# First product of the second feed-forward part by Strassen's scheme over two of its three input blocks

## The chip, the cores and the metric

The kernel runs on one core of a Trainium2 chip (trn2). The metric is the time of one execution on the device in microseconds; the time of a kernel is the median of its runs. Engines have the profile's short names: PE is the matrix engine TensorE, PEld its weight loads, DVE is VectorE, ACT is ScalarE, POOL is GpSimd, SP is SyncE, which issues the DMA transfers here.

## What is computed

A recurrent attention (4 sequences, 8 heads, 768 steps, 48 channels a head) gives 3072 tokens of 384 channels. A gated feed-forward part and a second one with Mish follow:

```python
def _moe_ref(x, w_gate, w_val, w_out) -> np.ndarray:
    gate = 1.0 / (1.0 + np.exp(-(x @ w_gate)))
    val = x @ w_val
    return (gate * val @ w_out).astype(np.float32)
...
def _moe2_ref(x, w_in, w_out) -> np.ndarray:
    h = x @ w_in
    sp = np.where(h > 20.0, h, np.log1p(np.exp(np.minimum(h, 20.0))))
    g = h * np.tanh(sp)
    return (g @ w_out).astype(np.float32)
```

The first part's weights are 384x1536 (twice) and 1536x384, the second's are 384x2048 (`w_in`) and 2048x384 (`w_out`).

## The kernel before

Every fp32 product is made of three fp16 ones: each factor is split into a high half and a rest, and high x high, high x rest and rest x high are summed in PSUM. The weights lie in DRAM as 64-bit words and are decoded on the chip into the two halves; the decoding of a chunk (`load_raw`, `decode`, L329) is a transfer, a few integer steps on ACT and DVE (L306, L350), a cast for the high half (L361) and a subtraction for the rest (L364). For `w_out` of the second part, `combine` (L378) also makes sums and differences of its blocks (L389), because that product already follows Strassen's scheme.

**First part.** It runs over 12 pairs (NP) of 256 tokens (NT). While attention for a later pair is computed on all engines, `gate` (L1116) makes the gate and value products of a pair (L1133), the sigmoid (L1144), their product (L1149) and its split (L1161, L1164), and `out1` (L1190) the next product (L1201). Its results go to DRAM as `x2d`, split in two halves.

**Second part.** It runs over 6 blocks (RB) of 512 tokens, two pairs each. `load_x2` fetches a block. `h_unit` (L1298) makes one column of 128 of the first product with 9 matmuls of 128x512 (3 input blocks x 3 terms, L1311) from weights that stay in SBUF, and ACT applies Mish to it in one step (L1322). There are 16 such units per block. `operands` (L1328) takes two of them and makes what the second product needs: four sums on POOL (L1345), and seven operands that `split2` splits into a high half on ACT (L1359) and a rest on DVE (L1364). `out2` (L1401) is the second product by Strassen's scheme, 14 units of 24 matmuls of 128x192 per block (L1426), each with an evacuation on ACT or DVE (L1439, L1441). In block 0 the units of the first product alternate with the last pair's `out1` units; later with the `out2` units of the block before.

**What sets the order.** All work is registered as tasks with engines, costs in microseconds, and keys that they read and write. The class `Plan` gives each a due time, worked out backwards from the end, and a simulated clock then hands each engine the ready task that is due first (`run`, L115; `schedule`, L140). The result is a fixed order per engine; at run time each engine, SP's DMA queue among them, goes through its own list and waits on semaphores. `tail_end` (L1568) registers the decoding of the second part's weights; before, the chunks of `w_in` are decoded near the end of the first part, those of `w_out` across the border between the parts. The main loop is at L1599 to L1648.

## Time and profile before

| | before |
|---|---|
| median of 3 runs | 918.23 us (917.8 to 918.44) |
| profiled execution | 919.56 us |
| its span in the profile | 917.8 us |
| PE busy | 866.2 us, 94% |
| DVE busy | 633.6 us, 69% |
| POOL busy | 506.4 us, 55% |
| ACT busy | 490.7 us, 53% |

The span is what the profile covers; 1.76 us of the profiled execution lie around it, and this execution is 1.33 us above the median. Matrix products overlap their own filling and draining, so the duration shown for one matmul is longer than its distance to the next; prices are read from pieces of a chain instead.

### The profile page before, as it was taken

Reading aid. Unit: us, or ns where it says so; the run is one execution under the profiler, and the core shown is the slowest. Engines: PE = TensorE matmul, PEld = TensorE weight load, DVE = VectorE, ACT = ScalarE, POOL = GpSimd, SP = SyncE. Lnnn points to the kernel's source line nnn. Section 1 sums busy time; section 2 is a strip of 40 time slices with the busy share of each in tenths; the row PEclk is TensorE's granted clock in tenths of the full one; section 3 lists DMA queues with packets and bytes.
Section 4 is the critical chain, followed back from the end, with each engine's and each line's share of the span. In section 5 each row is a group of like instructions: output and inputs, shape, how many; then the busy total and the mean of one; then the engine's idle time right before and its main releaser. Section 6 shows DMA issues by size and latency. Waiting matters only on the chain.

```text
span 917.8 us, 29861 instructions
## 1 busy us (share of the span) xinstructions
PE 866.2 (94%) x13064; PEld 701.3 (76%) x13064; DVE 633.6 (69%) x1098; ACT 490.7 (53%) x1125; POOL 506.4 (55%) x562
## 2 busy tenths in 40 slices
PE   0578899999999999999999999999999999999998
PEld 0456788888888888888888885577677676776788
DVE  7897898877585777767688768765655655556541
ACT  2687854363543525262548777764655655556540
POOL 7996976646557474847553476543533434335320
PEclk9998999999999999999999999999999999999999
DMA  9277633222322232332306910100101002000001
GB/s 333 88 240 250 226 102 101 69 71 71 99 84 60 80 87 75 69 91 54 79 23 189 260 47 13 43 5 10 61 1 46 25 1 70 1 27 10 2 35 36
DMA packets 55315, 74.29 MB, mean 81 GB/s; under 512 B 19600, under 2 KB 36496, under 8 KB 55056
## 3 DMA queue, kind: packets, MB, share of 16 engines
q1 hardware_dynamic: 55184, 72.38, 26.3%
q8 instruction: 102, 1.67, 0.8%
q14 instruction: 29, 0.24, 0.1%
HBM read 58.99 MB, written 9.44 MB: 75 GB/s over the span
## 4 chain that ended last, share of the span: by engine, by line
PE 85%; POOL 4%; DVE 4%; ACT 3%; DMA 2%; issue 1%; SPq 0%; DVEq 0%; ACTq 0%; POOLq 0%
PE gv L1133 27%; PE h L1311 20%; PE o L1426 18%; PE o L1201 14%; PE yp L1013 3%; POOL pt L546 2%; PE kp L910 2%; POOL blk L546 1%; ACT KK L851 1%; ACT X L716 1%; PE lp L695 1%; POOL wos L364 1%; DMA raw_wv<-wv 1%; DVE A L566 1%; PE kt L806 0%
## 5 line engine op out<-in xcount | busy, mean ns | idle before, releaser
L1311 PE MATMUL h<-x,wis 128*128 128x512 f16 x864 | 199.9, 379 | 0.0
L1345 POOL TENSOR_TENSOR sum<-e 128x256 f32<-128x256 f32 x96 | 71.9, 748 | 179.9 <-ACT e L1322 179.9
L1133 PE MATMUL gv<-xt,wgs 128*128 128x256 f16 x1296 | 166.5, 274 | 4.8 <-DVE gt L1164 3.1
L1133 PE MATMUL gv<-xt,wvs 128*128 128x256 f16 x1296 | 165.6, 275 | 2.1 <-ACT sig L1144 1.8
L1201 PE MATMUL o<-gt,wos 128*128 128x256 f16 x1296 | 163.5, 273 | 0.0
L1311 PEld LDWEIGHTS <-wis 128*128 128x128 f16 x864 | 83.5, 98 | 82.9
L1133 PEld LDWEIGHTS <-wgs 128*128 128x128 f16 x1296 | 125.5, 98 | 21.7 <-issue 4.7
L1133 PEld LDWEIGHTS <-wvs 128*128 128x128 f16 x1296 | 126.4, 99 | 19.3 <-issue 2.2
L546 POOL TENSOR_TENSOR blk<-blk 128x384 f32<-128x384 f32 (+4 forms) x151 | 123.2, 829 | 30.1 <-DMA blk<-rkw 11.9
L1201 PEld LDWEIGHTS <-wos 128*128 128x128 f16 x1296 | 125.8, 98 | 17.9 <-issue 0.2
L546 POOL TENSOR_TENSOR pt<-blk 128x384 f32<-128x384 f32 x93 | 105.6, 1160 | 35.8 <-DMA blk<-rkw 33.1
L1322 ACT ACTIVATE e<-h 128x512 f32<-128x512 f32 x96 | 57.3, 597 | 85.9 <-PE h L1311 84.9
L1149 DVE SCALAR_TENSOR_TENSOR gv<-gv,sig 128x512 f32<-128x512 f32 x72 | 50.6, 703 | 54.2 <-ACT sig L1144 26.2
L1144 ACT ACTIVATE sig<-gv 128x512 f32<-128x512 f32 x72 | 42.1, 596 | 81.8 <-PE gv L1133 81.5
L1161 ACT CAST gt<-gv 128x512 f16<-128x512 f32 x72 | 42.2, 585 | 67.7 <-DVE gv L1149 67.5
L1426 PE MATMUL o<-wps,gt 128*128 128x192 f16 x612 | 74.0, 246 | 0.0
L887 POOL TENSOR_TENSOR s<-s,WD 128x384 f32<-128x384 f32 x40 | 37.1, 936 | 55.6 <-DVE s L939 35.7
L851 ACT COPY KK<-KT 32x192 f32<-32x192 f32 (+1 forms) x168 | 59.9, 357 | 10.9 <-DVE KT L836 8.5
L1364 DVE SCALAR_TENSOR_TENSOR gt<-e,gt 128x256 f16<-128x256 f32 x41 | 27.5, 683 | 49.6 <-ACT gt L1359 49.6
L1426 PE MATMUL o<-wps,wgs 128*128 128x192 f16 x498 | 59.4, 246 | 0.0
L1164 DVE TENSOR_TENSOR gt<-gv,gt 128x512 f16<-128x512 f32 x72 | 49.3, 685 | 13.2 <-ACT gt L1161 12.9
L1426 PE MATMUL o<-wps,wos 128*128 128x192 f16 x456 | 57.1, 246 | 0.0
(123 smaller groups left out, 1461.8 us busy)
## 6 DMA issues: line engine op xcount, KB each, us to landing
v<-vt SPq DMA_DIRECT2D x24, 480.0 KB, 4.1
blk<-rkw SPq DMA_DIRECT2D x22, 384.0 KB, 3.6
raw_wi<-wi SPq DMA_DIRECT2D x8, 768.0 KB, 5.7
raw_wp<-wo SPq DMA_DIRECT2D x8, 768.0 KB, 5.6
blk<-rkw SPq DMA_DIRECT2D x11, 512.0 KB, 4.3
raw_wg<-wg SPq DMA_DIRECT2D x6, 768.0 KB, 5.4
raw_wv<-wv SPq DMA_DIRECT2D x6, 768.0 KB, 5.4
raw_wo<-wo SPq DMA_DIRECT2D x6, 768.0 KB, 5.2
```

Of the source, the lines that this page charges most:

```text
L546: engines[e].tensor_tensor(out=pv, in0=a, in1=b, op=ALU.mult)
L851: nc.scalar.copy(out=to, in_=own)
L1133: nc.tensor.matmul(gps[p, i, o][:, h], w[:, a, kc, fs], xt[p][:, c, kc, :], start=(n == 0), stop=(n == 3 * KC - 1),)
L1144: nc.scalar.activation(out=sgs[p, i], in_=gps[p, i, 0], func=AF.Sigmoid, scale=1.0 / (SW * SX))
L1149: nc.vector.scalar_tensor_tensor(out=gps[p, i, 1], in0=gps[p, i, 1], scalar=SG / (SW * SX), in1=sgs.pop((p, i)), op0=ALU.mult, op1=ALU.mult,)
L1161: nc.scalar.copy(out=gt[p][:, 0, 2 * i : 2 * i + 2], in_=gps[p, i, 1])
L1164: nc.vector.tensor_tensor(out=gt[p][:, 1, 2 * i : 2 * i + 2], in0=gps[p, i, 1], in1=gt[p][:, 0, 2 * i : 2 * i + 2], op=ALU.subtract,)
L1201: nc.tensor.matmul(ops[p, c][:, :NT], wos[:, a, f, cs], gt[p][:, g, f, :], start=(f == 0 and n == 0), stop=(f == NF1 - 1 and n == 2),)
L1311: nc.tensor.matmul(hps[r, f], w2["wi"][:, a, kc, fs], x2[r][:, c, kc, :], start=(n == 0), stop=(n == 3 * KC - 1),)
L1322: nc.scalar.activation(out=es[r, f], in_=hps[r, f], func=AF.Mish, scale=ih)
L1345: engines[e].tensor_tensor(out=sums[0][:, n - 1], in0=a(), in1=b(), op=op)
L1426: nc.tensor.matmul(ops2[h, first], home(slots[r, i, name])[:, c, tsl], w2["wp"][:, a, w, i, :], start=(new and n == 0), stop=(n == 3 * NF2 ...
```

## The change

It makes the first product of the second part by Strassen's scheme (Winograd's form) over input blocks 0 and 1; the third is multiplied plainly. The unit of work is now a group: two pairs of columns of 128, so 2x2 blocks on the weights' side, and 4 groups per block of 512 tokens, 24 in all.

- **`h_group`** replaces `h_unit`. Eleven block products (seven of the scheme, four plain) x 3 terms x 2 column chunks are 66 matmuls of 128x256 per group. They go into three PSUM banks X, Y, Z in seven steps; between steps on one bank, ACT copies it once (`first`) and DVE adds it to what was read before (`total`, five times). Of the four results one leaves X, one Y and two Z. ACT applies Mish four times. Units of `out1` or of the last block's `out2` stand between the steps (`more`).
- **`token_sums`**, new, once per block: POOL makes the token side's sums (one step over 128x768, five over 128x256), ACT casts the high halves, DVE the rests. All matmuls of the block's groups wait for all of them.
- **`operands`** works on 512 columns at a time instead of 256, so sums, high halves and rests halve in number and double in width.
- **The weights** are no longer kept in SBUF. `combine_in`, new, makes the sums and differences while a chunk is decoded (four steps, two casts, two subtractions), and the 11 blocks in both halves are stored in DRAM (`wid`, 8 transfers of 704 KB). `load_w` fetches a group's 2 x 704 KB, double buffered, two groups ahead.
- **Where decoding is registered:** chunk i of `w_in` at pair 3 + i of the first part, chunks of `w_out` in `decode_out`. The output's staging buffers are now two instead of three, and the extra buffer for raw weights is gone.

The core of the diff:

```diff
+NG = NF2 // 4
+NK = 11
+WIN = [(3 + i, 8) for i in range(8)]
...
+        def differ(e):
...
+            for out, a, b, op in (
+                (t[:, 0], end[:, 0], end[:, 1], ALU.add),
+                (t[:, 3:], top[:, ::2], end[:, ::2], ALU.subtract),
+                (t[:, 1], t[:, 0], top[:, 0], ALU.subtract),
+                (t[:, 2], top[:, 1], t[:, 1], ALU.subtract),
+            ):
...
-    def h_unit(r, f):
...
-        add("pe", 1.95, sums, [*w, ("x2", r % 2)], [ps])
-        add("act", 0.62, unit, [ps, "table2", "open"], [E])
...
+    def load_w(n):
...
+            for i in range(2):
+                nc.sync.dma_start(out=t[:, i], in_=wid[2 * (n % NG) + i])
...
+    def token_sums(r):
...
+        add("pool", 1.9, whole, [X], [F, T])
+        for k, (out, a, b) in enumerate(
...
+            add("pool", 0.75, lambda e, a=(out, a, b): sub(e, *a), [X], [T, F] if k == 4 else [T])
...
+        for k, (src, cost) in enumerate(((T, 0.83), (F, 0.38))):
+            add("act", cost, lambda e, k=k: high(e, k), [src, ("xt", r % 2, 0, 0)], [("tt", r % 2, k, 0)])
+            add("dve", cost + 0.1, lambda e, k=k: rest(e, k), [src, ("tt", r % 2, k, 0)], [("tt", r % 2, k, 1)])
...
+    def h_group(r, g, fill):
...
+            reads = [W, ("x2", r % 2), *(("tt", r % 2, k, a) for k in range(2) for a in range(2))]
+            add("pe", 0.655 * len(pairs), go, reads, [ps])
...
+        sums(X, [("A11", "B11")], True)
+        add("act", 0.6, first, [X], [("raw", 2), *(("u", k) for k in range(3))])
+        sums(Y, [("S2", "T2")], True)
+        total(Y, 0, 1)
+        sums(Z, [("S1", "T1"), ("F1", "G1")], True)
+        if g:
+            more()
+        sums(X, [("A12", "B21"), ("F0", "G0")], False)
+        unit("11")
+        more()
+        sums(Y, [("S3", "T3")], False)
+        total(Y, 0, 2)
+        total(Z, 2, "22")
+        unit("22")
+        more()
+        sums(Y, [("A22", "T4"), ("F1", "G0")], False)
+        total(Y, 0, "21")
+        unit("21")
+        sums(Z, [("S4", "B22"), ("D", "G1")], False)
+        total(Z, 1, "12")
+        unit("12")
+        operands(r, g)
+        if g:
+            more()
+        if n + 2 < NG * RB:
+            load_w(n + 2)
...
+            for i, at in enumerate(WIN):
+                if at == (p, f):
+                    decode_in(i)
             if f == 0 and p >= NP - 1:
                 load_x2(0)
+                load_w(0)
                 load_x2(1)
+                load_w(1)
+                token_sums(0)
```

The order of the instructions changes on all engines, because the planner works on other tasks. Two places follow.

POOL at the border of the two parts, before: the decoding of `w_out` (L389; `wps` are its halves, `sum_wp` the block sums) runs straight into the sums of block 0's Mish results `e` (L1345).

```order
291 L389 TENSOR_TENSOR sum_wp_9569<-word_wp_9479 128x384
292 L389 TENSOR_TENSOR sum_wp_9569<-word_wp_9479,sum_wp_9569 128x192 x2
293 L389 TENSOR_TENSOR wps<-word_wp_9479,wps 128x2x192
294 L389 TENSOR_TENSOR wps<-word_wp_9408,wps 128x2x192
295 L389 TENSOR_TENSOR wps<-sum_wp_9569,wps 128x4x192
296 L389 TENSOR_TENSOR sum_wp_9696<-word_wp_9624 128x384
297 L389 TENSOR_TENSOR sum_wp_9696<-word_wp_9624,sum_wp_9696 128x192 x2
298 L1345 TENSOR_TENSOR sum_0_9112<-e 128x256 x2
299 L1345 TENSOR_TENSOR sum_0_9112<-sum_0_9112,e 128x256
```

The same place with the change (line numbers of the new code: L437 is the old L389; L407 is `differ` for the last chunk of `w_in`; L1371 and L1376 are the token sums, of block 0 and then of block 1):

```order
320 L437 TENSOR_TENSOR wps<-word_wp_9509,wps 128x2x192
321 L437 TENSOR_TENSOR wps<-sum_wp_9592,wps 128x4x192
322 L407 TENSOR_TENSOR sum_wi_9696<-word_wi_9643 128x128
323 L407 TENSOR_TENSOR sum_wi_9696<-word_wi_9643 128x256
324 L407 TENSOR_TENSOR sum_wi_9696<-sum_wi_9696,word_wi_9643 128x128
325 L407 TENSOR_TENSOR sum_wi_9696<-word_wi_9643,sum_wi_9696 128x128
326 L1371 TENSOR_TENSOR xf_9734<-x_0_9153 128x768
327 L1376 TENSOR_TENSOR tf_9735<-xf_9734,x_0_9153 128x256
328 L1376 TENSOR_TENSOR tf_9735<-tf_9735,x_0_9153 128x256
329 L1376 TENSOR_TENSOR tf_9735<-xf_9734,tf_9735 128x256
330 L1376 TENSOR_TENSOR tf_9735<-xf_9734 128x256
331 L1376 TENSOR_TENSOR xf_9734<-xf_9734,tf_9735 128x256
```

The token sums of block 0, which its first group waits for, come after the last of the decoding on POOL. The other seven chunks of `w_in` have been decoded by then: their rows (L407, L414) stand far ahead, among the work of pairs 3 to 6.

DVE in the second part, before: rests (L1364) and evacuations (L1441) only.

```order
829 L1441 SCALAR_TENSOR_TENSOR o_9680<-o_1_4_11356,u_1_11023 128x192
830 L1364 SCALAR_TENSOR_TENSOR gt_9291<-sum_5_11245,gt_9291 128x256
831 L1364 SCALAR_TENSOR_TENSOR wos<-sum_5_11245,wos 128x256
832 L1364 SCALAR_TENSOR_TENSOR wgs<-sum_5_11245,wgs 128x256
833 L1364 SCALAR_TENSOR_TENSOR wgs<-e,wgs 128x256
834 L1441 SCALAR_TENSOR_TENSOR o_9680<-o_1_2_11124,u_0_10973 128x192
```

The same engine with the change, at the start of a block (L1463 are totals, `up` what has been added up, L1533 rests, L1411 the rest of the token sums):

```order
864 L1608 SCALAR_TENSOR_TENSOR o_9683<-o_1_4_11695,u_1_11277 128x192
865 L1463 TENSOR_TENSOR up_11960<-h_2_11953,up_11960 128x512
866 L1533 SCALAR_TENSOR_TENSOR gt_8804<-sum_11837,gt_8804 128x2x256 x2
867 L1533 SCALAR_TENSOR_TENSOR wgs<-sum_11837,wgs 128x2x256
868 L1533 SCALAR_TENSOR_TENSOR gt_9383<-sum_11837,gt_9383 128x2x256
869 L1533 SCALAR_TENSOR_TENSOR wgs<-e,wgs 128x2x256
870 L1463 TENSOR_TENSOR up_11960<-h_2_11953,up_11960 128x512
871 L1463 TENSOR_TENSOR e<-h_3_11963,up_11960 128x512
872 L1463 TENSOR_TENSOR e<-h_2_11953,up_11960 128x512
873 L1533 SCALAR_TENSOR_TENSOR wos<-e,wos 128x2x256
874 L1463 TENSOR_TENSOR e<-h_3_11963,up_11960 128x512
875 L1411 TENSOR_TENSOR tt_11933<-tf_12027,tt_11933 128x768
```

Between the first and the second total of a group stand five rests of the group before, which wait for ACT's casts, and four of them for POOL's sums as well; PE goes on with bank Y (here `h_2`) only when the total has read it.

## Rows read from the trace of the kernel before

**Rows 1.** The page: busy time by engine, and PE's granted clock by slice.

```profile
PE 866.2 (94%) x13064; PEld 701.3 (76%) x13064; DVE 633.6 (69%) x1098; ACT 490.7 (53%) x1125; POOL 506.4 (55%) x562
...
PEclk9998999999999999999999999999999999999999
```

**Rows 2.** Windows; columns: stretch, length, busy PE, PEld, DVE, ACT, POOL, clock, DMA, GB/s.

```profile
150.00:300.00 150.00, 150.00 (x3096) 132.95 (x3095) 109.78 (x199) 69.84 (x185) 93.76 (x102) 1.00 0.29 78
...
550.00:600.00 50.00, 50.00 (x297) 28.66 (x296) 40.02 (x69) 36.73 (x90) 30.55 (x39) 1.00 0.09 27
600.00:850.00 250.00, 250.00 (x2045) 177.79 (x2042) 145.04 (x282) 141.06 (x327) 104.01 (x137) 1.00 0.07 23
850.00:900.00 50.00, 50.00 (x478) 40.44 (x477) 22.26 (x47) 20.95 (x49) 15.18 (x20) 1.00 0.05 17
900.00:918.00 18.00, 14.59 (x177) 14.36 (x175) 2.86 (x8) 0.00 (x0) 0.00 (x0) 1.00 0.12 45
```

**Rows 3.** Waits from 550 to 850 us: who waited for whom, total, times, longest.

```profile
POOL sum L1345 <- ACT e L1322: 156.6, 78, 3.2
```

**Rows 4.** The chain of waits; columns: start, us, work.

```profile
259.80 1.97 PE gv L1133 x18
...
769.27 5.83 PE h L1311 x27
775.10 1.98 PE o L1426 x24
```

**Rows 5.** Timeline of PE at the border of the parts; columns: start, us, instructions.

```profile
548.85 1.15 PE L1201 MATMUL o<-gt,wos 128*128 128x256 f16 x9
549.84 5.99 PE L1311 MATMUL h<-x,wis 128*128 128x512 f16 x27
```

**Rows 6.** Groups of instructions; columns: count | busy us, mean ns | idle before, releasers.

```profile
L1345 POOL TENSOR_TENSOR sum<-e 128x256 f32<-128x256 f32 x96 | 71.9, 748 | 179.9 <-ACT e L1322 179.9
...
L1322 ACT ACTIVATE e<-h 128x512 f32<-128x512 f32 x96 | 57.3, 597 | 85.9 <-PE h L1311 84.9
...
L1149 DVE SCALAR_TENSOR_TENSOR gv<-gv,sig 128x512 f32<-128x512 f32 x72 | 50.6, 703 | 54.2 <-ACT sig L1144 26.2 <-PE gv L1133 18.1 <-issue 8.8
...
L1345 POOL TENSOR_TENSOR sum<-e,sum 128x256 f32<-128x256 f32 x48 | 37.9, 790 | 3.8
...
L1364 DVE SCALAR_TENSOR_TENSOR gt<-sum,gt 128x256 f16<-128x256 f32 x61 | 31.5, 535 | 0.9 <-ACT gt L1359 0.8
...
L1364 DVE SCALAR_TENSOR_TENSOR gt<-e,gt 128x256 f16<-128x256 f32 x41 | 27.5, 683 | 49.6 <-ACT gt L1359 49.6
...
L1441 DVE SCALAR_TENSOR_TENSOR o<-o,u 128x192 f32<-128x192 f32 x36 | 12.7, 352 | 14.2 <-PE o L1426 14.2
...
L364 POOL TENSOR_TENSOR wvs<-word_wv,wvs 128x768 f16<-128x768 f32 x5 | 8.2, 1647 | 7.0 <-ACT wvs L361 7.0
...
L389 POOL TENSOR_TENSOR sum_wp<-word_wp 128x384 f32<-128x384 f32 x6 | 6.1, 1018 | 7.9 <-DVE word_wp L350 7.9
```

**Rows 7.** Timeline of POOL, then of DVE, in the second part.

```profile
658.69 0.90 POOL L1345 TENSOR_TENSOR sum<-e 128x256 f32<-128x256 f32 x1
...
658.93 0.94 DVE L1364 SCALAR_TENSOR_TENSOR gt<-sum,gt 128x256 f16<-128x256 f32 x1
659.80 0.41 DVE L1364 SCALAR_TENSOR_TENSOR wgs<-e,wgs 128x256 f16<-128x256 f32 x1
660.13 0.41 DVE L1364 SCALAR_TENSOR_TENSOR wgs<-sum,wgs 128x256 f16<-128x256 f32 x1
```

**Rows 8.** DMA issues (KB each, us to landing), then the window with the highest rate.

```profile
raw_wi<-wi SPq DMA_DIRECT2D x8, 768.0 KB, 5.7
...
blk<-rkw SPq DMA_DIRECT2D x1, 1280.0 KB, 8.2
...
515.00:525.00 10.00, 9.98 (x92) 8.80 (x91) 9.17 (x15) 8.87 (x16) 5.49 (x5) 1.00 1.12 343
```

**Rows 9.** Timeline of DVE: the last rest of the second part's weights.

```profile
554.19 0.96 DVE L389 TENSOR_TENSOR wps<-sum_wp,wps 128x768 f16<-128x768 f32 x1 [0.61 <-ACT wps L403]
```

More of the change, by code (lines that the diff above doesn't have):

```diff
@@ L41 @@
 NPT = 32
-NRAW = 1
 YPOS = (4, 7)
@@ L327, in load_raw, with decode @@
         add("sp", 2.2, go, reads, [("raw", slot)], lat=2.0)
-    def decode(key, dst, n, count, slot, reads, high_on, lo_on, halves=False, blocks=None):
+    def decode(key, dst, n, count, slot, reads, high_on, lo_on, combine=None, blocks=None):
         raw = ("raw", slot)
@@ L1266, in mixer_moe_kernel @@
     homes = []
-    spare = list(range(78))
+    spare = list(range(39))
     slots = {}
@@ L1328, in operands @@
-    def operands(r, i):
-        sb_ = ("sum", i % 2)
-        E = [("e", (NF2 * r + 2 * i + h) % 4) for h in range(2)]
-        sums = {}
-        def part(h, t):
-            return es[r, 2 * i + h][:, NT * t : NT * t + NT]
-        def source(name):
-            if name[0] == "S":
-                return sums[0][:, int(name[1]) - 1]
-            return part(int(name[1]) - 1, int(name[0]) - 1)
-        def new(e):
-            sums[0] = w2["h"].tile([128, 4, NT], F32, tag=f"sum{i % 2}", name=f"sum{r}_{i}")
-        def both(e, n, a, b, op):
-            engines[e].tensor_tensor(out=sums[0][:, n - 1], in0=a(), in1=b(), op=op)
-        def S(n):
-            return lambda: sums[0][:, n - 1]
-        def A(h, t):
-            return lambda: part(h, t)
-        def split2(name, reads):
+    tt = {}
@@ new lines, in operands, with both, S, A @@
+    def operands(r, g):
+        n = NG * r + g
+        E = {q: ("e", n % 2, q) for q in ("11", "12", "21", "22")}
+        sums = {}
+        def new(e):
+            sums[0] = w2["h"].tile([128, 4, 2, NT], F32, tag="sum", name=f"sum{n}")
+        def both(e, k, a, b, op):
+            engines[e].tensor_tensor(out=sums[0][:, k - 1], in0=a(), in1=b(), op=op)
+        def S(k):
+            return lambda: sums[0][:, k - 1]
+        def A(q):
+            return lambda: es[n, q]
+        def split2(name, src, reads):
@@ L1455, in out2 @@
         n = {0: 0, 1: 1, 2: 1}.get(w, 2)
-        reads = [("slot", slots[r, i, name], c) for i in range(NF2 // 2) for c in range(2)]
+        reads = [("slot", slots[r, g, name], c) for g in range(NG) for c in range(2)]
         reads += [("wp", i, a, n) for i in range(NF2 // 2) for a in range(2)]
@@ L1468, in out2 @@
             reads = [bank, O, U, *([("u", h, k)] if k else [])]
-            add("dve", 0.35, lambda e: scaled(e, o(t, half), u(k)), reads, [("o", r % 3, t, half)])
+            add("dve", 0.35, lambda e: scaled(e, o(t, half), u(k)), reads, [("o", r % 2, t, half)])
             if name != "S1":
@@ L1479, in out2 @@
         if h:
-            spare.extend(slots[r, i, name] for i in range(NF2 // 2))
+            spare.extend(slots[r, g, name] for g in range(NG))
     def consts(e):
```

292 lines of the change are left out of this document (202 added, 90 removed).

## The prediction

> **What bounds the kernel now.** I read the engines' totals first: TensorE (PE) is busy 94% of the span, and its granted clock is in the top tenth after the fourth slice; the other engines have 30% and more to spare [rows 1]. A total hides stages, so the windows come next, with what is to be seen in each: from 150 us to 850 us PE is busy in all but hundredths of a microsecond of every window, first part and second alike, while VectorE (DVE) has 73% in 150 to 300 and 58% in 600 to 850, and GpSimd (POOL) 63% and 42% [rows 2]. Only the tail from 900 us has idle time on PE, 3.4 us [rows 2]. So in the second part every microsecond of PE is a microsecond of the span, and work on other engines is free as long as PE never waits for it. The list of waits agrees: its longest row is POOL waiting for Mish results, and PE stands in none as the one that waits [rows 3]. Nothing can thus be gained by removing waits; a gain must come from shorter PE work, and a loss from a wait that is new.
>
> The sum below is made against the profiled execution, 919.56 us with a span of 917.8; the median is 918.23, 1.33 lower, and I carry the difference over to it. A change of 0.2%, some 1.8 us, is about what a measurement of this kernel can tell from none.
>
> **PE's work.** Removed: 864 matmuls of 128x512. The chain of waits has 27 of them in a row taking 5.83 us, 0.2159 each [rows 4]: 186.5 us. Added: 24 groups of 66 matmuls of 128x256, 1584. The first part runs this form, one weight load each, 18 in 1.97 us, 0.1094 each [rows 4]: 173.3 us. Difference **-13.2 us**, 0.55 per group, all on the path.
>
> Per block of four groups PE then has 4 x 66 x 0.1094 = 28.9 us and, unchanged, 14 units of the second product at 1.98 [rows 4], 27.7: 56.6 us in which the other engines must finish their share. Block 0 has out1 units as filling instead, mostly six: 28.9 + 6 x 0.98 [rows 5] + 1.98 = 36.8 us.
>
> **What DVE and POOL get per block.** Shown durations on DVE contain a drain: rests of 128x256 start every 0.33 us and show 0.41 [rows 7], so I take 0.08 off each. Added: 20 totals of 128x512 from PSUM and SBUF, like the gate's product at 0.70 [rows 6], 0.62 each, 12.4 us. Rests: 28 of 128x512 in place of 56 of 128x256; no row has that form with both inputs in SBUF, two halves of 0.33 bound it above at 0.66 and half the price, 0.33, below, and I take 0.62 as for the total: 17.4. Evacuations, unchanged: 10 of 0.35 less 0.08 [rows 6], 2.7. Rests of the token sums, 128x768 and 128x256: 0.96 [rows 9] less 0.08 plus 0.33, 1.2. DVE alone: 33.7 us. POOL: 16 sums of 128x512; that size is not in the trace, it lies between 384 columns at 1.02 and 768 at 1.65 [rows 6], a third of the way: 1.23, 19.7 us; token sums 1.65 + 5 x 0.75 [rows 6], 5.4: **25.1 us**. ScalarE has 20 of 0.60 (first copies and Mish) [rows 6], 28 casts like them, and little else: 30 us. Each alone fits into 56.6, even into 36.8.
>
> They do not run alone. A rest beside a POOL sum takes 0.94 us in place of 0.41 and ends after the sum; the next rests, with POOL idle, are back at 0.41 [rows 7]. Over the kernel, 192 rests fed from sums average 0.535 and 144 fed from Mish results 0.683 [rows 6]: 192 x 0.12 + 144 x 0.27 = 62 us lost to 147.7 us of POOL sums (71.9 and twice 37.9 [rows 6]), 42%. DVE work that reads PSUM does not spread so: the gate's product averages 0.70 in 72 with POOL as busy [rows 6]. At 42%, DVE would need 33.7 + 0.42 x 25.1 = 44.2 us a block, under 56.6 and over 36.8. The Trainium skill ("SBUF — State Buffer", section "Who interferes with whom") calls the port pair that VectorE and GpSimd share an exclusive lock: a VectorE instruction with two SBUF inputs and a GpSimd one that reads SBUF exclude each other, one with a single SBUF input is not concerned. The trace agrees (0.94 against 0.41, and 0.70 for the PSUM-fed ones), and the rule speaks against this change: the new sums are longer, and there are more of them per block; by it DVE would need between 43.7 us, when only rests and POOL add up, and 58.8, when nothing overlaps.
>
> **Where PE may wait.** By these durations I laid out a steady group: PE needs about 15 us with its four fills, and the bank that the last-but-one step adds to has been read by DVE some 1.2 us before PE comes to it. So no wait inside a block. At a block's start only three fills lie in a group, DVE has five rests between two totals, and POOL follows its sums with the token sums (the piece of DVE's order above shows it): a total may come 0 to 2.2 us late. Four such starts: 0 to 9 us, I take **+2.4**, since the lock holds for under half of POOL's time.
>
> Block 0 has two dangers. Group n+2's weights, 1.44 MB in two transfers, are asked for when group n is done. Size for size, 768 KB took 5.7 us and 1280 KB 8.2 [rows 8], which goes on to 8.8; at the best rate of the trace, 343 GB/s [rows 8], 4.2 us and some 2 of latency: 6.3 to 8.8 us. By its order PE has about 6 us of other work between in block 0, and 11 later. So 0 to 2.9 us each for groups 2, 3 and 4. And DVE's 44.2 us against 36.8: up to 7, of which a lag of one group (the operands' tiles are double) is absorbed. Together 0 to 10, I take **+3**.
>
> The start. PE's first-part work and the out1 units ahead of group 0 end at 549.84 + 5.9 = 555.7 (before, the first product began at 549.84 [rows 5]). Group 0 waits for the token sums, which POOL's order puts behind the decoding of the last weight chunk of both products. Before, that decoding ended with a rest at 554.2 + 0.96 = 555.2 [rows 9]. Two chunks fewer of the second product are left for this stretch in the new order, one of the first is added, and the token sums cost 1.65 + 5 x 0.75 on POOL and about 2 on the other engines. 0 to 7 us late, I take **+1**, as gained and added work nearly balance.
>
> The first part. The title says one chunk per pair; in the order seven of the eight chunks are decoded early, all among pairs 3 to 6, because the raw load waits for nothing but its buffer. That adds to POOL at most five times four sums (at most 0.75 each [rows 6], fewer columns most) and eight rests at 1.65 [rows 6], 26 us, and about 17 us to DVE, in some 150 us in which they had 56 and 40 us free [rows 2]. They feed the attention there, whose results PE's gate needs. 0 to 8 us, **+1**: PE had no wait in that window at all [rows 2], so there is slack of unknown size. The eight stores of 704 KB lie on SP's queue beside loads of a like size [rows 8]; the DMA share was 0.29 [rows 2]: nothing, or in the same 8 us if a load is late behind one.
>
> What falls away at the end of the first part (seven decodings) is hidden before already, so it gives nothing. The tail's 3.4 us stay: the last block's second product is unchanged.
>
> **Sum:** -13.2 + 2.4 + 3 + 1 + 1 = -5.8. Profiled 913.8, median **912.4 us**, 0.6% faster.
>
> **Rivals.** *A, all covers hold:* only the arithmetic remains, with at most 3 us of waits: 905 to 908. For it: the 42% and PE's fills. Against: group starts with 1.2 us of slack or none.
>
> *B, the second part goes from PE to DVE (slower).* If every microsecond of POOL shuts DVE out, a block takes 33.7 + 25.1 = 58.8 us: 2.2 over PE in five blocks, 11, and some 19 in block 0 (58.8 less 2.7 of evacuations against 36.8): -13.2 + 30 = +17, 935 us. It decides as soon as POOL shuts DVE out for (56.6 - 33.7) / 25.1 = 91% of its time. Against it the 42% measured; for it that each single pair in [rows 7] shows the lock, and that DVE's static order puts totals behind rests.
>
> *C, block 0 starves (no gain left).* Weights or operands there at the high end, +10, and the other terms as taken: -13.2 + 10 + 4.4 = +1.2, 919.4; with the start late as well, 922.
>
> *D, the first part pays.* Decoding delays attention at its high end: -13.2 + 8 + 6.4 = +1.2, 919.4. For it, POOL goes from 63% [rows 2] to some 80%; against, no wait of PE there now.
>
> **Chances.** Likeliest, stalls of 4 to 10 us, 908 to 916: 0.45. A 0.18, B 0.12, C 0.16, D 0.09. Faster by over 0.2% (under 916.4) are the likeliest, A and a piece of C: 0.65. Within: half of C and of D, 0.13. Slower: B and the rest, 0.22. The range leaves out B and the outer ends: 904.5 to 922.
>
> **What would show it.** Right: 1584 matmuls at 0.109 us apart; PE idle in the second part of some 6 us, at the starts of blocks waiting for totals on DVE and in block 0; the windows of 600 to 850 near 100% PE with DVE near 75%. A: no idle there. B: PE's idle spread over all groups, always for DVE, whose rests beside POOL take over 1.5 us. C: waits for the weight transfers, longer than 8 us each. D: PE idle between 150 and 330 us. Wrong altogether would be a matmul price other than 0.109 with new weights for each.

## The result and the profile after

| | before | changed |
|---|---|---|
| median | 918.43 us (6 runs) | 927.53 us (6 runs, 924.43 to 929.31) |
| ratio, 95% interval | | 1.0089 [1.0071, 1.0106] |
| profiled execution, its span | 919.56, 917.8 us | 929.31, 927.5 us |
| last gate matmul of the first part starts at | 548.7 us | 560.6 us |
| PE idle from 100 to 550 us | 3.3 us | 8.8 us |
| first group (before: first product) to last matmul, start to start | 364.5 us | 356.3 us |
| PE idle from 650 to 900 us | 0.0 us | 4.9 us |

The change is slower by 0.9%, where 0.6% faster was forecast. In every window idle time is its length less PE's busy time.

The page of the changed kernel, busy time by engine and granted clock by slice:

```profile
PE 859.8 (93%) x13784; PEld 774.7 (84%) x13784; DVE 708.9 (76%) x1079; ACT 484.8 (52%) x1005; POOL 553.6 (60%) x521
...
PEclk9998999999999999999999999999999999999999
```

PE is busy 6.4 us less than in [rows 1], though 13.2 us of matmuls were saved: what is left takes some 6.8 us longer. The span is 9.7 us longer. The windows (stretch, length, busy PE, PEld, DVE, ACT, POOL, clock, DMA, GB/s) say where:

```profile
150.00:300.00 150.00, 143.52 (x2767) 125.50 (x2767) 123.73 (x210) 85.24 (x201) 113.58 (x117) 0.98 0.52 147
...
550.00:600.00 50.00, 47.20 (x429) 41.80 (x429) 38.65 (x52) 29.31 (x50) 27.33 (x26) 1.00 0.29 104
600.00:850.00 250.00, 242.10 (x2550) 227.95 (x2548) 194.36 (x263) 134.16 (x239) 128.72 (x96) 1.00 0.37 127
850.00:900.00 50.00, 50.00 (x541) 47.65 (x540) 36.83 (x52) 25.76 (x45) 20.41 (x15) 1.00 0.21 75
```

Against [rows 2], PE has lost 6.5 us from 150 to 300, 2.8 from 550 to 600 and 7.9 from 600 to 850. The span splits at the first group. With nothing late it would start at 549.84 [rows 5] + 5.9 for the six out1 units now ahead of it, 555.7; it starts at 567.7, so the **first part is 12.0 us late**. PE's timeline there (start, us, instructions) has seven units of out1 between the last gate product and the first group, where one stood before:

```profile
559.70 1.15 PE L1181 MATMUL gv<-xt,wvs 128*128 128x256 f16 x9
560.68 7.15 PE L1249 MATMUL o<-gt,wos 128*128 128x256 f16 x63
567.67 0.82 PE L1440 MATMUL h<-x,wr 128*128 128x256 f16 x6
...
573.56 2.78 PE L1440 MATMUL h<-x,wr 128*128 128x256 f16 x24
```

From the first group to the last matmul it would take 364.5 - 5.9 - 13.2 = 345.4 us; it takes 356.3, so the **second part waits 10.9 us**. 12.0 - 13.2 + 10.9 = 9.7.

The price of a matmul came out as forecast. The chain of waits of the changed kernel, columns start, us, work:

```profile
704.38 2.62 PE h L1440 x24
707.00 1.98 PE o L1593 x24
```

24 in 2.62 us are 0.109 each, as in [rows 4].

**The first part.** The windows around the first stall, then PE's timeline in it:

```profile
180.00:190.00 10.00, 7.00 (x284) 5.91 (x284) 8.55 (x12) 2.57 (x6) 5.22 (x6) 1.00 1.04 226
190.00:200.00 10.00, 9.55 (x107) 7.88 (x95) 9.23 (x19) 9.14 (x29) 6.19 (x6) 0.83 0.33 114
```

```profile
185.80 0.49 PE L743 MATMUL lp<-RD,KD 64*32 64x48 f32 x34
189.25 1.07 PE L743 MATMUL lp<-RD,KD 64*32 64x48 f32 x94 [2.96 <-issue]
190.77 2.08 PE L1181 MATMUL gv<-xt,wgs 128*128 128x256 f16 x9 [0.45 <-DMA xt<-xs]
192.65 1.67 PE L1181 MATMUL gv<-xt,wvs 128*128 128x256 f16 x9
194.15 1.15 PE L1181 MATMUL gv<-xt,wgs 128*128 128x256 f16 x9
```

PE stops for 2.96 us inside a burst of attention's small products, for nothing that the profile shows, while the DMA engines are full (1.04). Then comes a second loss: nine gate matmuls that take 1.15 us take 2.08 and 1.67, and the granted clock of the window is 0.83. There is another such place at 290 us, with a granted clock of 0.83 from 290 to 300 us:

```profile
292.06 5.76 PE L1249 MATMUL o<-gt,wos 128*128 128x256 f16 x36 [2.29 <-DVE xo L279]
```

The 0.83 is a mean over a window of the clock's two levels, 1.2 and 2.4 GHz. Idle time before the first group grew by about 6 us; the other 6 of the 12.0 are work that takes longer. 3.1 us of that can be read behind the two waits: 27 gate matmuls take 4.5 us in place of 3.1, 36 of out1 5.8 in place of 4.1. Some more was lost from 95 to 105 us, where the clock is 0.83 against 1.00 before although PE's order there is still the old one; up to 166 us this leaves the changed kernel 0.5 us behind (its 541st gate matmul starts at 166.1 us, before at 165.6). So nearly all of the 12.0 us is lost after the point, at 171 us, where PE's order departs from that of before.

**The second part.** PE's list of waits from 540 us on, who waited for whom, total, times, longest:

```profile
PE h L1440 <- DVE up L1463: 7.6, 5, 2.2
PE h L1440 <- ACT up L1454: 1.2, 1, 1.2
...
PE h L1440 <- DMA wr<-wid: 0.8, 1, 0.8
```

One of these waits, at the start of a block, in the timelines of PE, DVE and POOL:

```profile
685.69 1.15 PE L1593 MATMUL o<-wps,wvs 128*128 128x192 f16 x12
689.09 2.78 PE L1440 MATMUL h<-x,wr 128*128 128x256 f16 x24 [2.25 <-DVE up L1463]
...
684.63 1.53 DVE L1533 SCALAR_TENSOR_TENSOR wvs<-sum,wvs 128x512 f16<-128x512 f32 x1
686.31 1.53 DVE L1533 SCALAR_TENSOR_TENSOR wgs<-sum,wgs 128x512 f16<-128x512 f32 x1
687.76 0.68 DVE L1533 SCALAR_TENSOR_TENSOR wgs<-e,wgs 128x512 f16<-128x512 f32 x1
688.36 0.68 DVE L1463 TENSOR_TENSOR up<-h,up 128x512 f32<-128x512 f32 x1
...
683.89 1.72 POOL L1516 TENSOR_TENSOR sum<-sum,e 128x512 f32<-128x512 f32 x1
685.69 1.60 POOL L1516 TENSOR_TENSOR sum<-e,sum 128x512 f32<-128x512 f32 x1
```

The total that PE needs stands in VectorE's order behind the rests of the group before. Two of them run beside POOL's sums and take 1.53 us; the next, with POOL idle, takes 0.68. Each of the two ends 0.55 us after the sum beside it. The Trainium skill ("SBUF — State Buffer", section "Who interferes with whom") says that a VectorE instruction with two SBUF inputs contends with a GpSimd one that reads SBUF, for a port pair that is an exclusive lock. These rows agree with it (1.53 us beside a sum, 0.68 alone).

### The profile page after: what moved, and what is told of

The parts are those of the page before. It is cut to its first block, busy times and chain, and to the rows that moved or that the text cites. A ratio compares the mean times of both kernels' runs of the same rounds, so it can differ in the third digit from the quotient of the medians.

```text
span 927.5 us, 31104 instructions
## 1 busy us (share of the span) xinstructions
PE 859.8 (93%) x13784; PEld 774.7 (84%) x13784; DVE 708.9 (76%) x1079; ACT 484.8 (52%) x1005; POOL 553.6 (60%) x521
## 4 chain that ended last, share of the span: by engine, by line
PE 69%; POOL 9%; DVE 7%; DMA 6%; ACT 6%; issue 2%; SPq 1%; ACTq 0%; POOLq 0%; DVEq 0%
PE gv L1181 25%; PE o L1249 13%; PE o L1593 12%; PE h L1440 12%; POOL sum L1516 3%; PE yp L1061 3%; DMA x<-x2d 3%; DMA xt<-xs 2%; POOL pt L594 2%; PE kp L958 2%; DVE sum_wp L437 1%; POOL tf L1376 1%; ACT KK L899 1%; ACT X L764 1%; POOL blk L594 1%
## 5 line engine op out<-in xcount | busy, mean ns | idle before, releaser
L1440 PEld LDWEIGHTS <-wr 128*128 128x128 f16 x1584 | 153.9, 98 | 27.7 <-issue 10.3
L1516 POOL TENSOR_TENSOR sum<-e 128x512 f32<-128x512 f32 x48 | 64.2, 1359 | 154.2 <-ACT e L1472 143.8
L1440 PE MATMUL h<-x,wr 128*128 128x256 f16 x1152 | 143.5, 273 | 9.7 <-DVE up L1463 7.6
L594 POOL TENSOR_TENSOR pt<-blk 128x384 f32<-128x384 f32 x93 | 108.6, 1192 | 15.8 <-DMA blk<-rkw 13.4
L1472 ACT ACTIVATE e<-e 128x512 f32<-128x512 f32 x72 | 45.0, 627 | 51.6 <-DVE e L1463 51.3
L1463 DVE TENSOR_TENSOR e<-h,up 128x512 f32<-128x512 f32 x72 | 49.3, 687 | 14.3 <-PE h L1440 13.4
L1440 PE MATMUL h<-tt,wr 128*128 128x256 f16 x432 | 59.4, 273 | 0.2 <-DVE e L1463 0.2
L1593 PE MATMUL o<-wps,gt 128*128 128x192 f16 x576 | 59.2, 246 | 0.0
L935 POOL TENSOR_TENSOR s<-s,WD 128x384 f32<-128x384 f32 x35 | 33.9, 974 | 41.1 <-DVE s L987 27.8
L614 DVE TENSOR_REDUCE A<-pt 128x32 f32<-128x768 f32 (+1 forms) x60 | 50.4, 861 | 5.7 <-POOL pt L594 5.7
```

The source lines that it names most:

```text
L594: engines[e].tensor_tensor(out=pv, in0=a, in1=b, op=ALU.mult)
L614: nc.vector.tensor_reduce(out=cell(), in_=shape(pts.pop(n)), op=ALU.add, axis=AX.X)
L1440: nc.tensor.matmul(banks[ps][:, i], wr[n][:, i, a, LEFT.index(w)], right(x, c), start=(new and i == 0 and k == 0 and j == 0), stop=(k == l ...
L1463: nc.vector.tensor_tensor(out=dst, in0=banks[ps], in1=ups[n][:, k], op=ALU.add)
L1472: nc.scalar.activation(out=es[n, q], in_=src, func=AF.Mish, scale=ih)
L1516: engines[e].tensor_tensor(out=sums[0][:, k - 1], in0=a(), in1=b(), op=op)
```

## The experiments

The last three columns are read from each run's profile. "Gate" is the start of the last gate matmul (the expectations call it the last gate product), the two idle times are PE's. The jobs follow in the order in which they ran; each theory is the one held at that time. The runs of one changed kernel scatter by 2 to 10 us, those of before by 3, so a time read from one profile carries as much.

| run | median us | ratio to before, 95% interval | gate, us | idle 100 to 550 | idle 650 to 900 |
|---|---|---|---|---|---|
| before | 918.43 | | 548.7 | 3.3 | 0.0 |
| the change | 927.53 | 1.0089 [1.0071, 1.0106] | 560.6 | 8.8 | 4.9 |
| one chunk per pair | 933.49 | 1.0161 [1.0134, 1.0188] | 561.8 | 9.4 | 5.7 |
| two chunks decoded | 927.52 | 1.0096 [1.0061, 1.0132] | 555.8 | 7.3 | 5.2 |
| transfers without arithmetic | 933.84 | 1.0163 [1.0134, 1.0191] | 565.2 | 14.9 | 6.0 |
| sums on VectorE | 937.29 | 1.0211 [1.0168, 1.0255] | 575.5 | 21.2 | 2.3 |
| all decoding late | 956.12 | 1.0395 [1.0361, 1.0430] | 571.0 | 16.3 | 5.0 |
| late, sums on VectorE | 943.99 | 1.0263 [1.0231, 1.0295] | 575.0 | 16.1 | 1.4 |
| late, token sums there too | 948.07 | 1.0324 [1.0302, 1.0347] | 569.3 | 16.3 | 1.5 |
| late, port told | 940.84 | 1.0240 [1.0214, 1.0265] | 582.8 | 16.1 | 1.2 |
| decoding off GpSimd | 938.26 | 1.0201 [1.0179, 1.0223] | 570.7 | 17.2 | 5.1 |
| one per pair, off GpSimd, port told | 920.72 | 1.0028 [1.0004, 1.0051] | 559.7 | 12.8 | 0.5 |
| port told | 940.24 | 1.0214 [1.0186, 1.0242] | 572.3 | 16.2 | 3.3 |
| one chunk decoded | 933.28 | 1.0152 [1.0104, 1.0201] | 555.9 | 7.8 | 5.6 |
| kernel before, transfers late | 929.93 | 1.0118 [1.0098, 1.0139] | 559.5 | 9.3 | 0.0 |
| same start, port told | 932.35 | 1.0146 [1.0116, 1.0177] | 569.4 | 16.6 | 2.7 |
| same start, sums on VectorE | 917.37 | 0.9986 [0.9973, 1.0000] | 558.0 | 7.2 | 1.1 |
| with look ahead | 920.58 | 1.0007 [0.9998, 1.0016] | 561.7 | 10.0 | 0.6 |
| look ahead, crowded | 924.56 | 1.0036 [1.0022, 1.0051] | 563.7 | 12.4 | 0.6 |
| look ahead, other table | 910.62 | 0.9899 [0.9884, 0.9913] | 552.3 | 6.4 | 0.0 |

### First job: decoding, transfers, sums

**One chunk per pair in fact.**

```diff
-        load_raw(key, lambda: dp, in_cols(wi, cs), (KC, 256), i % 2, [("x2d", WIN[i][0], KC - 1)])
+        load_raw(key, lambda: dp, in_cols(wi, cs), (KC, 256), i % 2, [("x2d", WIN[i][0] - 1, 1)])
```

The key in the change names a result that is not registered yet at that point, so the transfer waits for nothing; the edit names one that is.

> Edit: the transfer of weight chunk i waits for the results of the pair before, so that the chunks really are decoded one per pair, from the fourth pair on. Theory (the 12 us that the first part lost come from seven decodings crowded into pairs 3 to 6): the last gate product starts at 549 to 554 us instead of 560.7, the time falls to 917 to 922. Rival (any decoding added to the first part costs, wherever it stands): still 8 us or more late there, 924 or above.

The rival's numbers: the first part ends as late as in the change (561.8 us). Crowding alone is not the cause.

**Two of eight chunks decoded.**

```diff
-                nc.sync.dma_start(out=t[:, i], in_=wid[2 * (n % NG) + i])
+                nc.sync.dma_start(out=t[:, i], in_=wid[(2 * (n % NG) + i) // 7 * 7])
...
-                if at == (p, f):
+                if at == (p, f) and i in (0, 7):
```

> Edit: six of the eight chunks are neither loaded, decoded nor stored; the groups read chunk 0 (or 7) from DRAM in their place, so the second part does the same work. Theory (decoding and its transfers delay the first part): the last gate product starts at 548 to 552 us, the time is 915 to 919. Rival (the first part is late because its order was changed for another reason, or the second part carries most of the loss): above 923.

The rival's number. Without three quarters of the decoding the last gate product is still 4 us later than the latest expected, 7 later than before. It is 5 us earlier than in the change, but this profile is of the fastest of four executions and that of the change is of the slowest of six; by the medians both take 927.5 us.

**Their transfers alone.** Six raw loads and six stores go back in, with one small read of each raw tile on VectorE in place of the arithmetic:

```diff
+        if i in (0, 7):
             decode(
                 key, lambda: tiles[0], (KC, 256), i, i % 2, [stage], W3HI, W3LO, combine_in
             )
+        else:
+            add("dve", 0.1, lambda e: nc.vector.tensor_copy(out=junk, in_=raws[key][:, 0, :8, 1].bitcast(F32)), [("raw", i % 2)], [("junk", i)])
```

> Edit: as with two chunks decoded, but the six raw loads of 768 KB and the six stores of 704 KB stay (the stores write chunk 0); their arithmetic on GpSimd, VectorE and ScalarE is left out. Theory (the arithmetic on VectorE and GpSimd costs the time): as with two chunks, 915 to 919. Rival (the transfers stand in the way of those that attention waits for): 4 us or more above the kernel with two chunks, 921 to 928.

The rival's difference came, 6 us above the kernel with two chunks (the time itself lies above both ranges), and its place can be seen. PE's timeline and SP's queue:

```profile
200.29 2.10 PE L1182 MATMUL gv<-xt,wgs 128*128 128x256 f16 x9 [7.87 <-DMA xt<-xs]
...
182.30 3.73 SPq L1774 DMA_DIRECT2D wid<-made_wi  x4
...
187.34 5.86 SPq L1126 DMA_TRANSPOSE xt<-xs  x2
```

The tokens of the next pair are asked for behind four stores that without their arithmetic are ready at once, and behind two loads; PE waits 7.9 us for them. In the change the stores come one at a time, and PE's waits for such tokens are 2.0 us in all. So this run shows a danger, not what the change paid.

**The group's sums on VectorE.**

```diff
             add(
-                "pool",
-                1.2,
+                "dve",
+                0.65,
                 lambda e, k=k, a=a, b=b, op=op: both(e, k, a, b, op),
```

> Edit: the four sums per group for the second product go from GpSimd to VectorE; the token sums stay on GpSimd. Theory (PE waits for totals that stand in VectorE's order behind rests, which wait for GpSimd's sums and are shut out beside them): rests fall to 0.68 us each wherever no token sum runs, PE's idle time from 570 to 850 us falls from 10 us to under 5, the time to 919 to 923, the first part staying late. Rival (VectorE has too much to do, 43.6 us a block without being shut out, and the waits are its own): idle as before or more, 927 to 935.

The time missed both, because the first part became 15 us later still; the second part did what the theory said. Groups of rests (count | busy us, mean ns | idle before), first of the change, then of this run:

```profile
L1533 DVE SCALAR_TENSOR_TENSOR wos<-sum,wos 128x512 f16<-128x512 f32 x23 | 28.1, 1234 | 3.5 <-ACT wos L1530 2.9
```

```profile
L1533 DVE SCALAR_TENSOR_TENSOR wos<-sum,wos 128x512 f16<-128x512 f32 x23 | 15.6, 684 | 3.6 <-ACT wos L1530 3.6
```

From 1.23 to 0.68 us. From the first group to the last matmul it took 349.9 us in place of 356.3, though VectorE now does the sums as well: from 600 to 850 us they cost it 49.6 us, and its rests fall from 120.2 to 90.9. The 15 us in the first part come with no change to its work; only the order differs there.

### Second job: all decoding late

```diff
-        load_raw(key, lambda: dp, in_cols(wi, cs), (KC, 256), i % 2, [("x2d", WIN[i][0], KC - 1)])
+        load_raw(key, lambda: dp, in_cols(wi, cs), (KC, 256), i % 2, [("x2d", 7, KC - 1)])
```

The first kernel has this alone (and chunks registered at pair 9).

> Edit: the transfers of all eight weight chunks wait for the results of pair 7, so that nothing of the new decoding stands before about 440 us; the second part as in the change. New theory (attention for pairs 3 to 5, until about 200 us, has no slack for added work, and each wait there also lowers PE's granted clock; later there is slack): the last gate product starts at 548 to 553 us, the time is 914 to 919. Rival (the decoding costs as much anywhere, or the border takes it): first group 8 us or more later than 555.7, 924 or above.

The second has the group's sums on VectorE too.

> Edit: late transfers, and the four sums per group on VectorE. Theory (the two losses are separate: the first part's at 150 to 200 us, the second part's from sums on GpSimd; the second part took 362.4 us with them there and 356.0 with them on VectorE): second part 354 to 358 us, the time 907 to 912. Rival (what one stage gains the next gives back): 916 or above.

The third also puts the token sums of blocks 1 to 5 there.

> Edit: as the one before, and the token sums of blocks 1 to 5 on VectorE too, which leaves GpSimd idle in the second part. Theory (the waits left at the starts of blocks come from rests beside GpSimd's token sums): second part 351 to 355 us, the time 1 to 5 us under the kernel before it. Rival (VectorE's own load, some 46 us of 56.6 a block, makes the waits): equal or slower than the kernel before it.

The fourth has sums on GpSimd, and the planner is told of the port:

```diff
-            add("dve", 0.85, rest, [*reads, ("slot", k, 0)], [("slot", k, 1)])
+            add("dve", 0.65, rest, [*reads, ("slot", k, 0)], [("slot", k, 1)], port=True)
```

> Edit: late transfers, sums on GpSimd as in the change, but the planner is told that the rests share their port with GpSimd (cost 0.65 alone, slowed when GpSimd runs). Theory (totals stand behind rests because the planner takes these for shorter than they are beside GpSimd): totals come earlier in VectorE's order, second part 355 to 360 us, the time 2 to 7 us under the first kernel of this job. Rival (the total work of VectorE and GpSimd on one port is too much, whatever the order): within 2 us of the first kernel.

The theory of this job fell: all four are 21 to 37 us slower than before. The first three came out as their rivals had it; the fourth, 15 us faster than the first, lies outside both of its ranges. The first parts of the four differ by up to 14 us, so the differences in time are not the second part's alone. From 100 to 475 us PE is idle for 6 to 9 us, more than the 3.3 of before though nothing is decoded there; then 16 chunks of both products crowd the border, with 16 to 23 us of idle time from 475 to 650. For the second part's steady blocks the job is clean, since nothing there depends on where the decoding was: 5.0 us idle with the sums on GpSimd, 1.4 and 1.5 with them on VectorE, 1.2 with only the planner told. The token sums' place makes no difference in these blocks.

### Third job: what is left in the first part

GpSimd free of the new decoding, which goes to VectorE, and the raw weights of the second product later:

```diff
-W3LO = {"pool": 1.65, "dve": 0.92}
+W3LO = {"dve": 0.92}
...
-        add({"pool": 2.4, "dve": 1.4}, 0, differ, [word], [low])
+        add({"dve": 1.4}, 0, differ, [word], [low])
...
-            load_raw(("wp", i), lambda: dp, in_rows(wo2, cs), (2, DM), i % 3)
+            load_raw(("wp", i), lambda: dp, in_rows(wo2, cs), (2, DM), i % 3, [("x2d", 8, KC - 1)])
```

> Edit: the new decoding's sums and rests may go to VectorE alone, not to GpSimd, and the transfers of the second product's raw weights wait for pair 8 (so none of their sums stands on GpSimd in the first part); the chunks stay crowded early, the second part as in the change. Theory (GpSimd's in-order queue carries attention's chain to PE, and decoding steps ahead of it make PE wait at 150 to 300 us): the last gate product starts at 549 to 556 us instead of 560.7, the time is 915 to 922. Rival (VectorE's queue has no slack either): 560 or later, 927 or above.

The rival's number: 10 us later than the change in the first part. In this order VectorE's queue had no more room than GpSimd's.

The same with one chunk per pair and the planner told of the port:

> Edit: as the one before, and the chunks really one per pair, and the planner told that the second part's rests share a port with GpSimd. Theory (spread thin on VectorE it disturbs least; totals come earlier in VectorE's order): last gate product at 549 to 555 us, from it to the last matmul 353 to 358 us instead of 363.4, the time 908 to 915. Rival (spread means that every pair is disturbed): last gate product at 558 or later, 918 or above.

The second part as the theory had it (355.2 us from the last gate product, 348.2 from the first group, 0.5 us idle in the steady blocks), the first part and the time as the rival had them; the two nearly cancel against the saved matmuls.

The change with the planner told of the port, alone:

> Edit: the change with the planner told of the port in the second part's rests, nothing else. Theory (order, not the amount of work, makes the waits in the second part): from the first group to the last matmul 347 to 351 us instead of 356.3, and the first part late by about as much as in the change: 917 to 924. Rival (the late start of the kernel with late decoding gave its second part that length): 355 to 358 us, 925 to 931.

The rival's 356 us for the second part, and a time above both ranges. Idle time in the second part fell from 9.8 to 7.0 us, but the granted clock fell too, to 0.89 from 610 to 625 us and again from 695 to 710, where it was 1.00 in the change. The first part, in which nothing but the order differs, is 11.7 us later than in the change. Over four kernels, telling the planner leaves 0.5 to 3.3 us idle in the steady blocks: a help, not a sure cure.

Only the last chunk decoded, and read by all groups:

```diff
-                if at == (p, f):
+                if at == (p, f) and i == 7:
...
-                nc.sync.dma_start(out=t[:, i], in_=wid[2 * (n % NG) + i])
+                nc.sync.dma_start(out=t[:, i], in_=wid[7])
```

> Edit: only the last of the eight chunks is decoded, all groups read it, and the raw weights of the second product wait for pair 8: no decoding is left in the first part before about 480 us. Left out: seven decodings with their transfers. Theory (decoding work inside the attention's queues is what delays the first part): last gate product at 547 to 551 us, as in the kernel before. Rival (the changed second part alters the first part's order through the due times): 555 or later.

The rival's number. With no decoding of the second part's weights left before 480 us, the first part is 7 us late all the same. What it does have is another order: the early transfers and steps of the weights are gone, and the order of the engines departs from that of the kernel before from about 105 us on.

### Fourth job: the order itself

The kernel before, with nothing changed but a wait of eight transfers:

```diff
-            load_raw(("wi", i), lambda: dp, in_cols(wi, cs), (KC, 256), i % 3)
+            load_raw(("wi", i), lambda: dp, in_cols(wi, cs), (KC, 256), i % 3, [("x2d", 7, KC - 1)])
```

> Edit: the kernel before, in which only the transfers of the eight chunks of the second part's first weights wait for the results of pair 7; no work is added, taken away or changed. It takes three early transfers and some early steps on ScalarE and VectorE out of the first 200 us, and the planner's order differs from there on, much as in the kernel with one chunk. Theory (the first part's order in the kernel before fits the chip's real durations closely; any new order of the same work costs several us there): last gate product at 552 to 560 us instead of 548.7, the time 921 to 930. Rival (it is added work only): 548 to 550, 917 to 920.

The theory's number, and the clearest run of all: ratio 1.0118 [1.0098, 1.0139] with the same work on all engines. The second part takes 364.5 us as before; all of the loss is ahead of it. The windows, before and then two of this run:

```profile
100.00:200.00 100.00, 96.78 (x2027) 85.15 (x2025) 86.81 (x146) 56.44 (x140) 67.88 (x67) 1.00 0.40 112
```

```profile
100.00:200.00 100.00, 93.00 (x1848) 80.37 (x1847) 79.65 (x133) 50.52 (x131) 65.12 (x64) 0.96 0.26 68
200.00:440.00 240.00, 238.91 (x4819) 211.55 (x4818) 167.80 (x292) 96.03 (x252) 145.74 (x162) 1.00 0.28 76
```

The delayed transfers begin at 445 us. The 649th gate matmul starts at 196.1 us, before at 186.5: 9.6 of the 10.8 us are lost early, where this run has less to do than the kernel before. So it is not the work that was moved to a later place that costs them. PE's timeline at one of the waits, before and in this run:

```profile
119.33 3.11 PE L1201 MATMUL o<-gt,wos 128*128 128x256 f16 x27
123.75 2.12 PE L1133 MATMUL gv<-xt,wgs 128*128 128x256 f16 x18 [1.31 <-DVE gt L1164]
```

```profile
122.07 1.15 PE L1201 MATMUL o<-gt,wos 128*128 128x256 f16 x9
126.82 4.00 PE L1133 MATMUL gv<-xt,wgs 128*128 128x256 f16 x18 [3.61 <-DVE gt L1164]
```

The same two stages wait for the same tile, 3.61 in place of 1.31 us, and the 18 matmuls after it take 4.00 in place of 2.12. A wait of 2.3 us more has cost 4.2.

The change with its early transfers and words kept, so that the order of the first 165 us is that of the kernel before, and the decoding's other steps later, with the port told:

```diff
+T = (3, 3, 4, 4, 5, 6, 6, 7)
-        decode(key, lambda: tiles[0], (KC, 256), i, i % 2, [stage], W3HI, W3LO, combine_in)
+        decode(key, lambda: tiles[0], (KC, 256), i, i % 2, [stage, ("x2d", T[i], KC - 1)], W3HI, W3LO, combine_in)
```

> Edit: the change with the first two chunks' transfers and words as early as they come (the order of the first 165 us is then that of the kernel before), but sums, casts, subtractions and stores of the chunks wait for the results of pairs 3, 3, 4, 4, 5, 6, 6, 7; and the planner told of the shared port in the second part's rests. Theory (early order kept, decoding moved behind the stretch at 175 to 200 us): no idle time over 1 us on PE there, last gate product at 551 to 556 us, from it to the last matmul 354 to 358 us, the time 908 to 916. Rival (every re-planned stretch costs, wherever the decoding stands): last gate product at 559 or later, 917 or above.

The same with the sums on VectorE:

> Edit: as the one before, with the four sums per group on VectorE. Theory (the second part has its waits from GpSimd beside VectorE, and both cures work on the same waits): from the last gate product to the last matmul within 2 us of the kernel before it; the time differs by what the first part's order does. Rival (the cures add up): 351 to 353 us there.

The early order held, and the first of the two still lost, after 175 us. The second, whose first part has the same work to do, starts its last gate product 11 us earlier and is the first kernel not above the one before: 0.9986 [0.9973, 1.0000], which the noise does not tell from equal. From the last gate product to the last matmul it takes 353.3 us, 2.6 less than the other's 355.9: more than the theory's 2, and just above the rival's range.

### Fifth job: a planner that looks ahead

On top of the last kernel, a step of the new decoding is not started on an engine when a task of an earlier due time is about to arrive within its duration:

```diff
+            for r in ranked:
+                t = r[3]
+                if t.fill and any(
+                    e in n.cost and not n.fill and n.late < t.late and at < now + t.cost[e] - 0.1
+                    for n, at in etas[now].items()
+                    if n.end is None and n not in queues[e]
+                ):
+                    continue
+                return r[1:]
```

> Edit: the kernel with the same start and the sums on VectorE, in which the planner looks 3 us ahead: a sum, cast or subtraction of the new weight chunks does not start on an engine when a more urgent task of that engine is about to arrive within its duration. Theory (steps of 1 to 2.5 us, started just ahead of urgent ones on a queue that cannot be interrupted, make attention late): last gate product at 551 to 556 us instead of 558.0, the time 910 to 915. Rival (the planner's durations differ too much from the chip's for that to help): 557 or later, 916 or above.

With the chunks as early as they come:

> Edit: the same look ahead, with the chunks decoded as early as they come, as in the change, and the second part with the sums on VectorE and the port told. Theory: the crowded decoding costs less when it gives way, last gate product at 552 to 558 us, the time 911 to 917. Rival: 560 or later as in the change, 919 or above.

With the first kernel's chunks after the results of pairs 3, 3, 3, 4, 5, 5, 6, 7:

> Edit: as the first of this job, with chunks 0 to 7 after the results of pairs 3, 3, 3, 4, 5, 5, 6, 7. Any difference to the first is a different order of the same work. Theory (a new order of the same work alone moves the time by several us): 3 us or more from the first, either way. Rival: within 2 us of it.

Looking ahead did not help by itself (the rivals' numbers, in the first two). The first and the third do the same work by the same rules, only two chunks may start a pair earlier, and they are 10 us apart: 920.58 and 910.62. Most of that arises from 475 to 500 us, where PE is idle for 4.3 us in the first, mostly for ScalarE's copies KK (L948), and for none in the third. The third beats both kernels: 0.9899 [0.9884, 0.9913]. Its windows:

```profile
550.00:600.00 50.00, 49.48 (x462) 44.38 (x461) 39.26 (x65) 30.86 (x55) 4.35 (x6) 1.00 0.30 103
600.00:850.00 250.00, 250.00 (x2649) 236.56 (x2647) 207.84 (x342) 137.46 (x246) 24.33 (x24) 1.00 0.38 134
```

VectorE is busy 83% of the time and PE never waits. From the first group to the last matmul it takes 351.6 us with none of the out1 units ahead; 364.5 - 13.2 = 351.3, so 0.3 us of waits are left and the saved matmuls are all there. Its first part is 3.6 us late, with all eight chunks decoded in it.

## Why the prediction was wrong

**The matmuls: right.** -13.2 us, at 0.109 us each, and the last run has them in its time.

**The first part: the step that failed.** The four terms for waits came to 7.4 us and 22.9 were measured; 11 of the 15.5 between them are this term. "PE had no wait in that window at all [rows 2], so there is slack of unknown size", 0 to 8 us, taken as +1. It was 12.0, beyond even the bound of rival D. A full PE row says that the order fits, not that it has slack: the kernel before, planned anew with the same work, loses nearly as much (last gate late by 10.8 us), and the change with nothing altered but the cost and the port of the rests as the planner knows them ("port told") ends its first part another 11.7 us later. With six of the eight decodings left out the median is the same as that of the change, without any of them before 480 us 7 us are left, and with all of them in a lucky order 3.6. The loss is therefore put down to the order, not to the 26 and 17 us of added work that the prediction counted. That the order alone can cost this much is shown; how the 12.0 us divide between order and work is not, as no run keeps the order and takes only work away. Left out altogether was that a wait of PE can cost it clock afterwards, 3.1 of the 12.0 us behind two waits. How much a new plan moves was not to be read from the profile of before; that the planner re-plans all of the program was.

**The starts of blocks: mechanism right, size wrong.** Four waits at 628, 689, 747 and 805 us, on VectorE's totals behind rests beside GpSimd, as described: 6.5 us, 7.7 with one of 1.2 at 621 us for ScalarE's copy, taken as 2.4 within 0 to 9. The sums took 1.36 to 1.56 us on average, not 1.23 (alone 1.27), and a rest beside them up to 1.76, where 0.62 was taken. The average was not too low: 168 rests took 163 us, some 8 us a block more than at 0.68 each, where 42% of 25.1 gives 10.5. But with four of them ahead of a total, what one total waits for does not even out, as the 42% supposed.

**Block 0 and the start: about right.** Some 2 us of waits in block 0 (1.1 for a total, 0.8 for weights) where 3 were taken, none at the first group where 1 was. The two weight transfers of groups 2 and 3 landed 6.0 and 7.0 us after the first of the two was issued, at the lower end of the 6.3 to 8.8 estimated. The waits of the second part add up to 9.8 us of idle time; the other 1.1 of its 10.9 are an estimate of what filling up again costs, as nine matmuls are shown as 1.15 us and start every 0.98.

**Rival B:** the second part did not go to VectorE, whose share was 78% from 600 to 850 us. What decided was a total's place in the order, not the sum of both engines' times; with the sums moved to VectorE its share rises to 82 and 83% (first and last of these kernels) and the idle time from 650 to 900 us falls from 4.9 us to between 2.3 and 0.0.

Not settled: what PE waited for in the 2.96 us at 186 us ("issue"; in it the profile has one 16 KB transfer of instructions beside full DMA engines, and no run tests whether PE waited for that), and which of the many displaced steps makes an order good or bad; the runs show the spread, not a rule for it.

## What to carry to other kernels

Where one planner orders the whole program, a change in one part is paid in all: re-plan the old kernel once with nothing changed but a wait that does no harm, and see how far its time moves, before a difference is put down to the change. An engine that is busy without a gap may be a well-fitted order rather than a stage with room. Where VectorE and GpSimd work on one stream of tiles, moving GpSimd's share to VectorE can cost VectorE less than that share's own time (here 49.6 us of sums, while its rests became 29.3 us shorter), and what stands ahead of a step that PE waits for matters more than the totals of engine time.

## What was not expected of the hardware

- A short wait of PE can cost more than itself: 2.96 us of waiting in the change were followed by 18 matmuls at 2.08 + 1.67 us in place of 2.3; in the re-planned kernel before, 2.3 us more of waiting cost 1.9 us more in the 18 matmuls behind it. It need not: behind the wait of 2.25 us at 689 us 24 matmuls take 2.78 us, as 24 do without a wait at 574 us, and the clock stays at 1.00.
- Beside each other, VectorE and GpSimd both slow down in the changed kernel: rests of 128x512 from 0.68 to 1.53 us and more (up to 1.76), GpSimd's sums from 1.27 to 1.7.
- With six loads and six stores and no arithmetic between them ("transfers without arithmetic"), PE waited 7.9 us for tokens whose transposing transfers were issued behind four stores of 704 KB and two loads; they took 10.8 us to land (median of two), before 4.0.
